# An attention decode kernel on one core: the output projection's weight in 1 MB blocks, two of them ahead of the last V piece

## The chip, the cores and the metric

The kernel runs on one core of a Trainium2 chip. The metric is device time in microseconds (us), lower is better. One execution of each kernel was also recorded by the hardware profiler; its span is about 1.7 us shorter than the time that is scored (the kernel before: span 1354.6 us, scored 1356.3 us in that run). All times inside a trace count from the start of the span. The engines are named as the profile names them: PE multiplies matrices (PEld is its loading of weights), DVE, ACT and POOL do the rest of the arithmetic, SP issues the transfers; DMA are the 16 engines that move the data. A block of "1 MB" is 2^20 bytes; the profile's own MB are decimal.

## The reference

Cut to what matters: a gated mix of a cached attention step and a small feed-forward block, for 4 tokens (D = 1024, 32 heads of 128, 8192 cached keys).

```python
g = sigmoid((x * gate_w).sum(-1, keepdims=True))
q = (x @ wq).reshape(B, 1, 32, 128).transpose(0, 2, 1, 3)
p = softmax(einsum("bhqd,bhkd->bhqk", q, k_cache) * 128 ** -0.5)   # k_cache: 4 x 32 x 8192 x 128 bf16
o = einsum("bhqk,bhkd->bhqd", p, v_cache)
a = o.reshape(B, 1, 4096) @ wo                                     # wo: 4096 x 1024 bf16, 8 MB
out = g * a + (1 - g) * b                                          # b: the feed-forward block
```

K and V are 256 MB each. Everything is read once, 575.7 MB in all, and little is computed on it.

## The kernel before

All large loads go through one ring of five SBUF slots of 4 MB. A load may start when the slot's earlier user is done. SP issues all of them, in program order.

```python
ring = ctx.enter_context(tc.tile_pool(name="ring", bufs=5))

def slot():
    return ring.tile([P, RING], BF, name="piece", tag="piece")

def wo_piece(g0, g1, r0=0, r1=FR):            # blocks g0..g1 of wo; one block is 1 MB, 8 matmuls of 512 columns
    ng, nr = g1 - g0, r1 - r0
    w = slot()[:, :ng * nr * D].rearrange("p (g r n) -> p g r n", g=ng, r=nr)
    nc.sync.dma_start(out=w.rearrange("p g r n -> p g (r n)"),
                      in_=wov[:, g0:g1, r0:r1].rearrange("p g r n -> p g (r n)"))
    def use():
        for g in range(ng):
            for r in range(nr):
                for n in range(NH):
                    mm_acc(acc[:, n * NB:(n + 1) * NB], LT[:, r0 + r, g0 + g, :], w[:, g, r, n * NB:(n + 1) * NB])
    return use
...
for u in range(NT + LAG):                      # NT = 64 pairs of heads, LAG = 4
    if u < NT:
        k_piece(u)
    if u >= LAG:
        v_piece(u - LAG)                       # the last V piece is fetched in four quarters
    ...
    if u == NT:
        o_rows(0, GE)                          # GE = 6: LT for wo blocks 0 to 5 is ready early
        add_x()
GS = NWB // 2                                  # NWB = 8 blocks
last = [wo_piece(0, GS), wo_piece(GS, GE), wo_piece(GE, NWB - 1),
        wo_piece(NWB - 1, NWB, 0, FR - 1), wo_piece(NWB - 1, NWB, FR - 1, FR)]
flush()                                        # the last heads: oT, OT
o_rows(GE, NWB)                                # LT for blocks 6 and 7 needs the last V piece
for use in last:
    use()
# then acc goes to SBUF in two halves (DVE, ACT) and out in two small DMAs
```

`acc` is the PSUM tile in which the output is summed, and `LT` holds the attention's result, transposed to be the weights of the wo matmuls. So wo comes as pieces of 4, 2, 1, 0.75 and 0.25 MB, all behind the last V piece, and PE's first wo matmul waits for all of the 4 MB.

## Time and profile before

| | before |
|---|---|
| time, median of 4 runs | 1355.85 us (1355.29 to 1356.14) |
| span of the profiled run | 1354.6 us |
| last landing of the last V piece | 1325.4 us |
| landing of the 4 MB wo piece | 1335.4 us |
| last wo landing | 1345.3 us |
| last matmul ends | 1351.7 us |

First from the page of the kernel before, the slices of DMA (the mean busy share of the 16 DMA engines in tenths, 40 equal slices), and its DMA queues (packets, MB, share of the 16 engines' span):

```profile
DMA  9999999999999999999999999999999999999996
...
q1 hardware_dynamic: 21904, 575.69, 99.0%
q8 instruction: 40, 0.66, 0.2%
```

The DMA engines are busy from end to end (99.0% of the span on q1). What can be won without moving fewer bytes lies where PE still works after the data has come. The timeline of PE in the kernel before shows that end (start us, us, engine, line, operation, out<-in, partitions x elements, count, and the idle time before it with what ended it). L342 are the last V matmuls, L355 and L232 the softmax tail, L150 the wo matmuls:

```profile
1325.63 3.19 PE L342 MATMUL o_ps<-piece,PB_143 128*8 128x512 bf16 x14
1329.54 1.06 PE L355 MATMUL oT<-selg,OS_139 128*128 128x8 f32 x8 [0.72 <-ACT OS_139 L348]
1330.93 0.33 PE L232 MATMUL o_ps<-OT,identb 128*32 128x8 bf16 x16 [0.33 <-DVE OT L358]
1335.42 16.26 PE L150 MATMUL acc<-piece,LT 128*4 128x512 bf16 x64 [4.16 <-DMA piece<-in_A_wo_dram]
```

PE waits 4.16 us for the 4 MB piece and then runs 64 matmuls in one go for 16.26 us. Windows of 2 us of the same stretch (busy time and instruction count of PE, PEld, DVE, ACT, POOL, then the granted PE clock, the DMA share and GB/s):

```profile
1332.00:1334.00 2.00, 0.00 (x0) 0.00 (x0) 0.00 (x0) 0.00 (x0) 0.00 (x0) 0.81 1.02 426
1334.00:1336.00 2.00, 0.58 (x2) 0.21 (x2) 0.00 (x0) 0.00 (x0) 0.00 (x0) 0.50 1.00 416
1336.00:1338.00 2.00, 2.00 (x7) 0.57 (x5) 0.00 (x0) 0.00 (x0) 0.00 (x0) 0.50 0.90 373
1338.00:1340.00 2.00, 2.00 (x6) 0.57 (x5) 0.00 (x0) 0.00 (x0) 0.00 (x0) 0.50 0.69 285
1340.00:1342.00 2.00, 2.00 (x10) 0.77 (x9) 0.00 (x0) 0.00 (x0) 0.00 (x0) 0.98 0.56 227
...
1346.00:1348.00 2.00, 2.00 (x11) 0.77 (x9) 0.00 (x0) 0.00 (x0) 0.00 (x0) 1.00 0.00 0
```

Two things are to be seen. The clock is at 0.50 from 1334 to 1340 us, so only 9 matmuls start from 1336 to 1340 us, one every 427 ns, where 18 start from 1344 to 1348, one every 216 ns (the counts in the windows are higher, because they include matmuls that reach in from the window before). And from 1346 us on nothing is fetched any more (DMA share 0.00) while PE works on until 1351.7.

The DMA share falls by steps from 1336 us on (0.90, 0.69, 0.56), long before the last byte. The reason shows in the records of completion. In this trace every large transfer has 16 such records, and they are spread out. I read them as one from each of the 16 DMA engines; a record does not name its engine, but the share of 0.56 from 1340 to 1342 us is that of nine busy engines of 16. Read so, these are the times at which engines were done with the last V quarter and the 4 MB piece, in us:

```
last V quarter   first 1317.3   seventh 1320.4   eighth 1323.8   last 1325.4
4 MB of wo       first 1327.3   seventh 1330.3   eighth 1333.8   last 1335.4
```

Seven engines are done 5 to 8 us before the slowest. The transfer has landed for PE when the slowest engine is done with it: the last record of the 4 MB is at 1335.4 us, and the first matmul on them starts at 1335.42.

### The profile page before, as it was taken

How to read it: one execution, taken by the hardware profiler on the slowest of the kernel's cores; microseconds unless marked ns; L12 is line 12 of the kernel's file. 1: busy time of each engine (PE TensorE's matmuls, PEld its weight loads, DVE VectorE, ACT ScalarE, POOL GpSimd, SP SyncE). 2: the span in 40 equal slices, each digit the busy share in tenths (PEclk: the TensorE clock that was granted, in tenths of full speed). 3: DMA queues.
4: the chain of work that ended last, by engine and by line, in shares of the span. 5: the costliest groups of instructions: out<-in, count | busy, mean ns of one | idle time of the engine just before them, and what ended most of it. 6: DMA issues, size and time to landing. Idle time of an engine off the chain costs nothing.

```text
span 1354.6 us, 11809 instructions
## 1 busy us (share of the span) xinstructions
PE 1065.1 (79%) x5112; PEld 434.5 (32%) x5112; DVE 622.3 (46%) x403; ACT 71.0 (5%) x118; POOL 86.8 (6%) x326
## 2 busy tenths in 40 slices
PE   2775888888687878879787777868877787888797
PEld 2432333333233323333233333323333332333333
DVE  1553345544543554455355534545454445445500
ACT  0000000000000000000000000000000000000010
POOL 2000000000000000000000000000000000000000
PEclk9877998889899988989999898989989888998898
DMA  9999999999999999999999999999999999999996
GB/s 403 429 431 430 425 430 432 432 432 431 429 432 430 433 430 431 427 431 432 431 433 432 433 428 432 430 428 433 431 433 430 432 428 430 432 431 433 432 419 258
DMA packets 21976, 576.46 MB, mean 426 GB/s; under 512 B 2322, under 2 KB 2330, under 8 KB 2596
## 3 DMA queue, kind: packets, MB, share of 16 engines
q1 hardware_dynamic: 21904, 575.69, 99.0%
q8 instruction: 40, 0.66, 0.2%
q14 instruction: 12, 0.10, 0.0%
q10 hardware_dynamic: 20, 0.02, 0.0%
HBM read 575.69 MB, written 0.01 MB: 425 GB/s over the span
## 4 chain that ended last, share of the span: by engine, by line
DMA 47%; PE 31%; DVE 12%; issue 7%; POOL 2%; ACT 1%; DVEq 0%; SPq 0%; ACTq 0%
DMA piece<-in_A_k_cache_dram 45%; PE o_ps L342 16%; PE S_ps L286 12%; DVE T L279 10%; DMA piece<-in_A_wo_dram 3%; PE acc L150 2%; PE oT L355 1%; DVE PT L311 1%; PE shr L150 1%; POOL PB_142 L316 1%; POOL PB_143 L316 1%; POOL tot L320 0%; ACT OS_138 L348 0%; ACT OS_139 L348 0%; DVE OT L358 0%
## 5 line engine op out<-in xcount | busy, mean ns | idle before, releaser
L279 DVE STREAM_TRANSPOSE T<-piece 128x2048 uint32<-128x2048 uint32 x256 | 576.1, 2288 | 474.7 <-DMA piece<-in_A_k_cache_dram 370.0
L286 PE MATMUL S_ps<-T,Z_140 128*128 128x512 bf16 x1024 | 287.9, 436 | 164.9 <-DVE T L279 164.6
L286 PE MATMUL S_ps<-T,Z_141 128*128 128x512 bf16 x1024 | 259.1, 401 | 84.1 <-DVE T L279 83.8
L342 PE MATMUL o_ps<-piece,PB_143 128*8 128x512 bf16 x1024 | 226.5, 381 | 2.1 <-POOL PB_143 L316 2.1
L342 PE MATMUL o_ps<-piece,PB_142 128*8 128x512 bf16 x1024 | 226.2, 379 | 0.0
L286 PEld LDWEIGHTS <-Z_140 128*128 128x128 bf16 x1024 | 111.3, 109 | 337.2 <-issue 256.4
L286 PEld LDWEIGHTS <-Z_141 128*128 128x128 bf16 x1024 | 102.1, 101 | 239.8 <-issue 143.6
L342 PEld LDWEIGHTS <-PB_143 128*8 128x8 bf16 x1024 | 86.5, 87 | 139.9 <-issue 15.3
L342 PEld LDWEIGHTS <-PB_142 128*8 128x8 bf16 x1024 | 86.4, 87 | 137.3 <-issue 13.6
L358 DVE SCALAR_TENSOR_TENSOR OT<-oT,sgb,rinv 128x8 bf16<-128x8 f32 x16 | 3.8, 236 | 126.0 <-PE oT L355 126.0
L270 POOL COPY Z_141<-qa 32x4 bf16<-32x4 bf16 x128 | 25.1, 196 | 525.1 <-PE S_ps L286 519.5
L270 POOL COPY Z_140<-qa 32x4 bf16<-32x4 bf16 x128 | 25.1, 196 | 496.4 <-PE S_ps L286 482.5
L348 ACT COPY OS_138<-o_ps 8x512 f32<-8x512 f32 x32 | 18.5, 577 | 594.2 <-PE o_ps L342 594.2
L348 ACT COPY OS_139<-o_ps 8x512 f32<-8x512 f32 x32 | 18.5, 577 | 536.8 <-PE o_ps L342 536.8
L150 PE MATMUL shr<-xw,piece 128*128 128x4 bf16 x704 | 22.6, 170 | 2.8 <-DMA piece<-in_A_wq_dram 2.6
L150 PEld LDWEIGHTS <-piece 128*128 128x128 bf16 x704 | 22.6, 113 | 3.9 <-DMA piece<-in_A_wq_dram 2.7
L150 PE MATMUL acc<-piece,LT 128*4 128x512 bf16 x64 | 16.3, 421 | 4.2 <-DMA piece<-in_A_wo_dram 4.2
L322 DVE RECIPROCAL rinv<-tot 128x8 f32<-128x8 f32 x16 | 3.2, 203 | 25.6 <-POOL tot L320 25.6
L355 PE MATMUL oT<-selg,OS_139 128*128 128x8 f32 x64 | 8.5, 259 | 5.7 <-ACT OS_139 L348 5.7
L355 PE MATMUL oT<-selg,OS_138 128*128 128x8 f32 x64 | 8.5, 259 | 5.7 <-ACT OS_138 L348 5.7
L316 POOL COPY PB_143<-PT 64x512 bf16<-64x512 bf16 x8 | 8.3, 1032 | 65.9 <-DVE rex L318 65.9
L150 PE MATMUL acc<-piece,hT 128*4 128x512 bf16 x56 | 12.4, 379 | 0.0
(99 smaller groups left out, 145.9 us busy)
## 6 DMA issues: line engine op xcount, KB each, us to landing
piece<-in_A_k_cache_dram SPq DMA_DIRECT2D x64, 4096.0 KB, 39.7
piece<-in_A_v_cache_dram SPq DMA_DIRECT2D x63, 4096.0 KB, 38.7
piece<-in_A_wq_dram SPq DMA_DIRECT2D x2, 4096.0 KB, 13.5
piece<-in_B_w_gate_dram SPq DMA_DIRECT2D x2, 3584.0 KB, 39.9
piece<-in_B_w_up_dram SPq DMA_DIRECT2D x2, 3584.0 KB
piece<-in_B_w_down_dram SPq DMA_DIRECT2D x1, 4096.0 KB, 39.9
piece<-in_A_v_cache_dram SPq DMA_DIRECT2D x4, 1024.0 KB, 38.4
piece<-in_A_wo_dram SPq DMA_DIRECT2D x1, 4096.0 KB, 39.4
```

The source lines that it names most:

```text
L150: nc.tensor.matmul(out_ap, lhsT=lhsT, rhs=rhs, start=start, stop=True, skip_group_check=True)
L270: nc.gpsimd.tensor_copy(out=Z[32 * a:32 * a + 32, :, 31 + 32 * a:32 + 32 * a], in_=qa[32 * a:32 * a + 32, :, h0 + a // QH, b:b + 1])
L279: nc.vector.transpose(out=T[:].rearrange("p j h i e -> p (j h i e)").bitcast(U32), in_=kn[:, c * CJ * Dh:(c + 1) * CJ * Dh].bitcast(U32))
L286: nc.tensor.matmul(sps[:, :], lhsT=Z[:, he, s:s + P], rhs=T[:, 16 * jl:16 * jl + 16, half, :, e], start=(t == 0 and jc == 0 and he == 0), ...
L311: nc.vector.transpose(out=PT[:].rearrange("p j i -> p (j i)"), in_=PTs[:])
L316: nc.gpsimd.tensor_copy(out=B_[W:P, :, :, 1, :], in_=Pv[W:P])
L322: nc.vector.reciprocal(out=rinv[:], in_=tot[:])
L342: nc.tensor.matmul(o_ps[32 * t:32 * t + NM, :], lhsT=B_[:, JC * t + jc, uq].rearrange("p s j -> p (s j)"), rhs=vn[:, j0 * Dh:(j0 + 4) * Dh ...
L348: nc.scalar.copy(out=o_sb[32 * t:32 * t + NM, :], in_=o_ps[32 * t:32 * t + NM, :])
L355: nc.tensor.matmul(oT[:, :], lhsT=o_sb[:, q * Dh:(q + 1) * Dh], rhs=selg[:, q].rearrange("p t s -> p (t s)"), start=(q == 0), stop=(q == 3))
L358: nc.vector.scalar_tensor_tensor(out=OT[:, hg:hg + GH, b], in0=oT[:, :], scalar=sgb[:, 1, b:b + 1], in1=rinv_t.pop(g)[:], op0=ALU.mult, op ...
```

## The change

The intent: wo comes in blocks of 1 MB, each waited for by its own 8 matmuls alone, so that matmuls start with the first block and run while later ones land; and two blocks go ahead of the last V piece, so that their 16 matmuls run before V's.

```diff
@@ -377,9 +377,11 @@
         if u == NT:
             o_rows(0, GE)
             add_x()
-    GS = NWB // 2
-    last = [wo_piece(0, GS), wo_piece(GS, GE), wo_piece(GE, NWB - 1),
-            wo_piece(NWB - 1, NWB, 0, FR - 1), wo_piece(NWB - 1, NWB, FR - 1, FR)]
+        if u == NT + LAG - 2:
+            for g in range(2):
+                wo_piece(g, g + 1)()
+    last = [wo_piece(g, g + 1) for g in range(2, NWB - 1)]
+    last += [wo_piece(NWB - 1, NWB, 0, FR - 1), wo_piece(NWB - 1, NWB, FR - 1, FR)]
     flush()
     o_rows(GE, NWB)
     for use in last:
```

The bytes, the 64 matmuls and the size of one contiguous run in DRAM (8 KB) stay. There are nine wo transfers in place of five.

## The prediction

> **What bounds the kernel.** The DMA queues. The slices show DMA at 0.9 or more in 39 of 40 slices; windows of the trace give 412 GB/s in 0–50 us and 430 GB/s from 100 to 1330 us, and 575.7 MB have to come. PE (79% busy) and DVE (46%) wait for data. The change moves the same bytes, so it can win only in the tail, where PE still works after the data has come.
>
> **The tail before, from timeline, waits and landings.** The last V piece's four quarters land at 1317.7, 1320.5, 1323.0 and 1325.4 us; the five wo pieces at 1335.4 (4 MB), 1340.3, 1342.8, 1344.6 and 1345.2 us. PE finishes V at 1328.8 and the last softmax rows at 1331.3, waits 4.2 us for the 4 MB piece (waits: "PE acc <- DMA wo", 4.2 us), then runs 64 matmuls from 1335.4 to 1351.7, 6.4 us past the last landing. About twelve of them start every 427 ns, the rest every 213 ns: the clock windows show 0.50 from 1334 to 1340 us. [...] counted on the trace, windows busy under about 0.4 fell and those above stayed fast, with few exceptions; the one before this drop was busy 0.32. The output then takes 2.9 us, to 1354.6.
>
> **What the change does.** 64 matmuls and 8 MB stay. Four more issues cost SP 0.33 us each, off the path. Two 1 MB blocks go ahead of the last V piece, so V's quarters land about 5 us later (1 MB takes 2.4–2.5 us here): estimated 1322.6 to 1330.4. Their 16 matmuls (3.4 us) fill PE after the piece before, which ends near 1322.7. V should end near 1332.7, the softmax tail near 1335.2, with no 4 us gap, so the clock should stay full. From there each block needs 8 × 0.213 = 1.7 us of PE against 2.45 us of DMA. The blocks land near 1332.9, 1335.4, 1337.9, 1340.3, 1342.8, the last two near 1344.6 and 1345.3; PE catches up with the fourth or fifth block and ends about 1.2 us after the last landing, 1346.5. Output: +2.9, span 1349.4. That is 5.2 us of 1354.6: half of it the clock (12 × 0.21 = 2.6 us), half the overlap of matmuls with landings.
>
> **Buffers.** Five slots. One-MB blocks use up slots with a quarter of the bytes. The last V piece now waits for the third piece before it (freed at 1307, still 13 us of data queued); blocks 4 and 5 of wo wait for blocks 0 and 1; block 6 waits for the V piece (1333), the last two for blocks 2 and 3 (1337, 1339). The slow DMA engines need them from 1340 on; the fast ones, about 8 us ahead, may idle, harmlessly. So I expect no bubble on the slow ones.
>
> **Predicted:** 1351 us, 8 in 10 between 1349.3 and 1354.5. Faster by over 2%: 0.01; within 2%: 0.97; slower by over 2%: 0.02.
>
> **What would show it.** Last landing still 1345–1346; first wo matmuls before V's; last matmul within 1.5 us of the last landing; clock windows 1.00 from 1320 to 1346; no DMA share under 0.9 before about 1335.
>
> **What would make it wrong.** A window that falls on the softmax tail drops the clock: half-speed blocks need 3.4 us each against 2.45, and most of the gain goes. Or slots come free late (release signals, landing of the previous use), the slow engines starve, and the last landing moves out by as much. Nothing before 1285 us should change.

The passage that is cut told a rule of the clock that did not come from the traces of this case. It carried no term of the sum, which stands as written: last matmul 1346.5, output 2.9, span 1349.4. A window is a stretch of 3.413 us: in the traces of the kernels before and after, each record of the granted clock (0.50 or 1.00) lasts a whole multiple of that, but for the one that the end of the trace cuts short. The count meant is this one, of the kernel before from 60 us on: 37 windows at full clock were followed by one at 0.50, and in 34 of them PE was busy for at most 0.42 of the window; 279 were not, and in all of them it was busy for 0.42 or more.

## The result, and the profile after

| | before | after |
|---|---|---|
| time, median of 4 runs | 1355.85 us (1355.29 to 1356.14) | 1351.32 us (1351.15 to 1351.37) |
| span of the profiled run | 1354.6 us | 1349.4 us |
| last V quarter landed | 1325.4 us | 1330.2 us |
| last wo landing | 1345.3 us | 1345.2 us |
| last matmul ends | 1351.7 us | 1346.5 us |

The ratio is 0.9967 with a 95% interval of 0.995 to 0.9984. Ratios here are the mean time of one kernel's fast runs over that of the other's fast runs of the same rounds, so not quite the ratio of the medians quoted. The gain, 4.5 us by the medians and 5.2 us of span in the profiled runs, is clear of the spread of either kernel but far under 2%.

From the page of the changed kernel, the same two lines as before:

```profile
DMA  9999999999999999999999999999999999999997
...
q1 hardware_dynamic: 21968, 575.69, 99.4%
```

The timeline of PE in the changed kernel. The first two lines are wo matmuls of the blocks ahead of V, of which there are 16, started from 1322.12 to 1325.4 us; the rest is the same end as before:

```profile
1322.12 0.38 PE L150 MATMUL acc<-piece,LT 128*4 128x512 bf16 x1
1322.77 2.32 PE L150 MATMUL acc<-piece,LT 128*4 128x512 bf16 x10
...
1325.80 6.30 PE L342 MATMUL o_ps<-piece,PB_143 128*8 128x512 bf16 x27
1332.82 1.06 PE L355 MATMUL oT<-selg,OS_139 128*128 128x8 f32 x8 [0.72 <-ACT OS_139 L348]
...
1334.54 5.12 PE L150 MATMUL acc<-piece,LT 128*4 128x512 bf16 x23
1340.21 1.89 PE L150 MATMUL acc<-piece,LT 128*4 128x512 bf16 x8 [0.55 <-DMA piece<-in_A_wo_dram]
1342.69 3.78 PE L150 MATMUL acc<-piece,LT 128*4 128x512 bf16 x16 [0.59 <-DMA piece<-in_A_wo_dram]
```

V and the softmax tail come about 3.3 us later than before, but the 4.16 us wait is gone. PE has caught up with the transfers at 1340 us: from there it does 8 matmuls in 1.9 us and waits twice more, 0.55 and 0.59 us, for the blocks that follow. Windows of the changed kernel, same columns as before:

```profile
1332.00:1334.00 2.00, 1.16 (x9) 1.07 (x9) 0.09 (x1) 0.58 (x1) 0.00 (x0) 1.00 0.98 352
1334.00:1336.00 2.00, 1.80 (x24) 0.84 (x24) 0.34 (x2) 0.00 (x0) 0.00 (x0) 1.00 0.97 406
1336.00:1338.00 2.00, 2.00 (x11) 0.77 (x10) 0.00 (x0) 0.00 (x0) 0.00 (x0) 1.00 0.82 301
1338.00:1340.00 2.00, 1.67 (x8) 0.59 (x7) 0.00 (x0) 0.00 (x0) 0.00 (x0) 1.00 0.88 353
1340.00:1342.00 2.00, 1.79 (x8) 0.67 (x8) 0.00 (x0) 0.00 (x0) 0.00 (x0) 1.00 0.79 325
1342.00:1344.00 2.00, 1.41 (x8) 0.51 (x7) 0.00 (x0) 0.00 (x0) 0.00 (x0) 1.00 0.52 210
1344.00:1346.00 2.00, 1.99 (x10) 0.74 (x9) 0.00 (x0) 0.00 (x0) 0.00 (x0) 1.00 0.13 48
1346.00:1348.00 2.00, 0.48 (x3) 0.00 (x0) 0.68 (x1) 0.57 (x1) 0.00 (x0) 1.00 0.01 4
```

The clock stays at 1.00, and PE is done about 1.3 us after the last landing. The landings, that is the last of the sixteen completion records of each transfer, in us, beside what the prediction had estimated:

```
                      V quarters                        blocks 2 to 6                              block 7 (two parts)
predicted    1322.6           ...      1330.4    1332.9  1335.4  1337.9  1340.3  1342.8    1344.6  1345.3
measured     1322.7  1325.2  1327.7   1330.2    1332.7  1335.1  1337.6  1340.2  1342.7    1344.6  1345.2
```

Three landings of the kernel before stand a little early in the prediction: its 1317.7, 1344.6 and 1345.2 are 1318.0, 1344.7 and 1345.3 when all sixteen records are counted. Nothing in its sum hangs on that.

### The profile page after: what moved, and what is told of

Read it like the earlier page. It is cut to its first block, busy times and chain, and to the rows that moved or that the text cites. A ratio compares the mean times of both kernels' runs of the same rounds, so it can differ in the third digit from the quotient of the medians.

```text
span 1349.4 us, 11817 instructions
## 1 busy us (share of the span) xinstructions
PE 1065.0 (79%) x5112; PEld 434.1 (32%) x5112; DVE 622.4 (46%) x403; ACT 71.0 (5%) x118; POOL 86.2 (6%) x326
## 4 chain that ended last, share of the span: by engine, by line
DMA 47%; PE 31%; DVE 11%; issue 8%; POOL 2%; ACT 1%; SPq 0%; DVEq 0%; ACTq 0%
DMA piece<-in_A_k_cache_dram 45%; PE o_ps L342 16%; PE S_ps L286 12%; DVE T L279 10%; DMA piece<-in_A_v_cache_dram 2%; PE oT L355 1%; PE acc L150 1%; DMA piece<-in_A_wo_dram 1%; DVE PT L311 1%; POOL PB_143 L316 1%; POOL PB_142 L316 1%; PE shr L150 1%; POOL tot L320 0%; ACT OS_138 L348 0%; ACT OS_139 L348 0%
```

## The experiments

Twelve kernels were run, in three batches. Those of a batch ran on the same chip and share their runs of the kernel before (medians 1356.65, 1355.93 and 1355.89 us; the first chip's runs of it fell in two groups, 1355.5 to 1355.8 and 1356.6 to 1356.9).

The theory: the gain is that PE's matmuls run while later transfers land, and that without the 4 us wait PE's clock does not drop; the last landing, set by the DMA engines, does not move. Rivals: the gain comes from the two blocks ahead of V; it is all clock, or no clock; it takes blocks as small as 1 MB.

### e1_split_only: all blocks behind V

Against the changed kernel:

```diff
-        if u == NT + LAG - 2:
-            for g in range(2):
-                wo_piece(g, g + 1)()
-    last = [wo_piece(g, g + 1) for g in range(2, NWB - 1)]
+    last = [wo_piece(g, g + 1) for g in range(0, NWB - 1)]
```

> All wo in 1 MB blocks, none ahead of the last V piece. My theory (the gain is that matmuls run while later blocks land, and that no 4 us gap drops the clock; the place of the two blocks does not matter): after the softmax tail at 1331.3 us two or three blocks have already landed, PE starts them at once at full clock, needs 64 x 0.213 = 13.6 us, i.e. could end at 1345, so it ends behind the last landing (1345.2) just as the changed kernel does: last matmul 1346.5, about 1351.3 us. Rival (the gain needs the two blocks ahead of V, which fill PE while it waits for V): 16 matmuls come back behind V, 3.4 us, about 1354.7 us.

Measured: 1351.16 us (1351.11 to 1351.27), span 1349.4. The theory holds, the rival falls: the place of the two blocks is worth nothing that shows. The PE timeline of e1_split_only has 47 wo matmuls in one run from 1331.74 us and then waits for blocks:

```profile
1331.74 10.30 PE L150 MATMUL acc<-piece,LT 128*4 128x512 bf16 x47
1342.64 3.77 PE L150 MATMUL acc<-piece,LT 128*4 128x512 bf16 x16 [0.59 <-DMA piece<-in_A_wo_dram]
```

By 1331.7 us two blocks lie there already, PE needs 1.7 us a block against 2.45 us between landings, and it has caught up before the last blocks. Here blocks 5 to 7 are issued as late as 1333.4 to 1338.6 us, because they wait for the slots of blocks 0 to 3. The fast DMA engines stood idle for that, as I read the records: the 16 of block 5 lie within 1.3 us (1338.8 to 1340.1) in place of 8. The last landing is at 1345.1 all the same. That was the prediction's "may idle, harmlessly".

### e2_ahead_only: two blocks ahead, a 4 MB piece behind

Against the changed kernel:

```diff
-    last = [wo_piece(g, g + 1) for g in range(2, NWB - 1)]
+    last = [wo_piece(2, GE), wo_piece(GE, NWB - 1)]
```

> The changed kernel with the two 1 MB blocks still ahead of V, but blocks 2 to 5 again as one 4 MB piece. My theory (waiting for a large piece is what costs): the 4 MB land at 1340.3, PE has waited 5 us and is at half clock again, 48 matmuls take about 12.8 us from there: last matmul near 1353, span 1356, about 1357.5 us, i.e. worse than the kernel before. Rival (what counts is having 16 matmuls fewer behind V): 1352.4 us.

Measured: 1357.47 us (1357.03 to 1357.93), ratio 1.0011. As expected, and by the medians slower than the kernel before, though the interval (0.9997 to 1.0025) still holds 1. From the PE waits of e2_ahead_only (engine, what it waited for, us in total, times, longest), and its timeline:

```profile
PE acc L150 <- DMA piece<-in_A_wo_dram: 5.6, 1, 5.6
```

```profile
1340.15 12.34 PE L150 MATMUL acc<-piece,LT 128*4 128x512 bf16 x48 [5.58 <-DMA piece<-in_A_wo_dram]
```

Sixteen matmuls fewer behind V do not help while the next matmul waits for four blocks at once: the 4 MB are complete only at 1340.1 us, 4.7 us later than in the kernel before, since the two blocks went first as well.

### e4_one_cut: the kernel before with one cut

Against the kernel before:

```diff
-    last = [wo_piece(0, GS), wo_piece(GS, GE), ...
+    last = [wo_piece(0, 2), wo_piece(2, GS), wo_piece(GS, GE), ...
```

> The kernel before with its 4 MB wo piece cut in two pieces of 2 MB, nothing else. My theory: the first 2 MB land near 1330.4, so PE has work at 1331.3 and stays at full clock; pieces land at 1330.4, 1335.4, 1340.3, 1342.8, 1344.6, 1345.2; 16 matmuls of 3.4 us after the third end at 1343.7, then 8, 6 and 2 more: last matmul near 1347.1, span 1350.0, about 1351.9 us, i.e. nearly all of the gain. Rival (it takes 1 MB blocks, each waited for alone): a good part of the gain is missing, 1353.5 us or more.

Measured: 1351.88 us (1351.76 to 1352.92). The time is the expected one to a tenth of a microsecond: this one cut of the 4 MB piece gives nearly all of the gain, 0.7 us less than e1_split_only on the same chip. Not everything went as in the sum, though. The profiled run was the slowest one (1352.92), and in it V ended 1.7 us later than expected and the clock did drop for one window, as its windows show (columns as before):

```profile
1328.00:1332.00 4.00, 3.28 (x19) 1.61 (x18) 0.00 (x0) 0.58 (x1) 0.00 (x0) 1.00 1.02 426
1332.00:1336.00 4.00, 3.67 (x27) 1.43 (x27) 0.43 (x2) 0.00 (x0) 0.00 (x0) 0.58 1.00 416
```

The other three runs, 1351.76 to 1351.97, have only a mean clock for the whole run, which can't show one window. They fit the sum without a drop; whether they had none is not shown.

### e5_ahead4 and e6_ahead6: more blocks ahead

Against the changed kernel, with 6 for 4 in e6_ahead6:

```diff
-            for g in range(2):
+            for g in range(4):
-    last = [wo_piece(g, g + 1) for g in range(2, NWB - 1)]
+    last = [wo_piece(g, g + 1) for g in range(4, NWB - 1)]
```

> Four 1 MB blocks ahead of the last V piece instead of two. My theory: V's quarters land 5 us later still (last near 1335.2), V's softmax tail ends near 1339.8, four blocks are left (32 matmuls, 6.8 us), PE ends near 1346.5 again: 1351.3 us, no change against two blocks. The last V piece then waits for the slot of the V piece before it (free at 1322.7) with the slow DMA engines having data until about 1325: if the issue comes too late for them, the last landing moves out from 1345.2 by the difference. Rival (more blocks ahead is better): under 1350.5 us.

Measured: 1352.98 us (1352.78 to 1353.81). Neither the theory's 1351.3 nor the rival's gain. Two things in the trace were not in the sum. The clock was at 0.50 for one window behind the softmax tail (1340.0 to 1343.4 us), and block 7 landed late: fifteen engines were done with its first part by 1344.6 us, one at 1345.5.

> Six blocks ahead of the last V piece, so only blocks 6 and 7 behind it. My theory: V lands last near 1340.2, its softmax tail ends near 1344.9, 16 matmuls (3.4 us) are then left: last matmul 1348.3, span 1351.2, about 1353.1 us, 1.8 us worse than two blocks ahead, with the last landing still at 1345-1346. Rival (more blocks ahead is better): under 1351 us.

Measured: 1353.54 us (1353.08 to 1354.56). As the theory has it: the softmax tail is done at 1345.1 and 16 matmuls follow, with the last one done at 1348.8. Block 7 landed late here too (1346.4 and 1346.9), but the matmuls of block 6 covered that: the 16 run without a gap.

So two blocks ahead of V do no harm that shows, and more of them do. With six, V's softmax tail has moved to the end; the loss with four has other causes, taken up under e10_ahead4_warm.

### e0_after_again and e7_small_tail: the last transfers smaller

e0_after_again is the changed kernel again, the yardstick of this batch.

> The changed kernel again, on the chip of the other three: 1351.3 us, last wo landing at 1345.2, last matmul end at 1346.5. It is the yardstick for the others of this call.

Measured: 1351.30 us (1351.14 to 1351.43), ratio 0.9965. Its profiled run (1351.39 us) happened to catch the risk that the prediction had named, a clock drop behind the softmax tail. Timeline and windows of e0_after_again:

```profile
1334.72 11.99 PE L150 MATMUL acc<-piece,LT 128*4 128x512 bf16 x47
```

```profile
1332.00:1336.00 4.00, 2.95 (x33) 1.87 (x32) 0.42 (x2) 0.58 (x1) 0.00 (x0) 0.97 0.94 371
1336.00:1340.00 4.00, 4.00 (x13) 1.24 (x11) 0.00 (x0) 0.00 (x0) 0.00 (x0) 0.60 0.82 297
1340.00:1344.00 4.00, 4.00 (x21) 1.57 (x19) 0.00 (x0) 0.00 (x0) 0.00 (x0) 1.00 0.73 295
```

The clock was 0.60 on average from 1336 to 1340 us. PE then worked without a wait and was done at 1346.7, 0.2 us later than in the profile with the full clock. The drop takes one window of 3.4 us, about half of which, 1.7 us, is lost (an estimate: in the kernel before, wo matmuls start every 427 ns at a clock of 0.50 and every 216 ns at 1.00); but without the drop PE stands waiting for blocks anyway (0.55 and 0.59 us in the timeline of the changed kernel), and the drop mostly eats those waits. Which of the two happens was luck: the activity of PE (the share of a window in which matmul columns stream, defined in the last section) was 0.41 in the window over the softmax tail here (1332.3 to 1335.8 us) and 0.43 in the changed kernel's first profile (1330.6 to 1334.0 us), where the clock stayed. By this count it hangs on where the windows of 3.4 us happen to fall.

e7_small_tail fetches blocks 6 and 7 into one slot, in smaller parts. Against the changed kernel, cut:

```diff
-    last = [wo_piece(g, g + 1) for g in range(2, NWB - 1)]
-    last += [wo_piece(NWB - 1, NWB, 0, FR - 1), wo_piece(NWB - 1, NWB, FR - 1, FR)]
+    last = [wo_piece(g, g + 1) for g in range(2, NWB - 2)]
+    tail = slot()[:, :2 * FR * D].rearrange("p (g r n) -> p g r n", g=2, r=FR)
+    def tail_piece(i, r0, r1):
+        nc.sync.dma_start(out=tail[:, i, r0:r1], in_=wov[:, NWB - 2 + i, r0:r1])
+        ...                                   # use(): the matmuls of rows r0 to r1 of block 6 + i
+    last += [tail_piece(0, 0, 2), tail_piece(0, 2, 4)] + [tail_piece(1, r, r + 1) for r in range(FR)]
```

> The changed kernel with wo blocks 6 and 7 in one slot, fetched as two transfers of 512 KB and four of 256 KB. My theory (PE has a backlog of 0.7 us at the last landing because block 7 comes as 6 + 2 matmuls): PE now ends with the last two matmuls 0.6 to 0.7 us after the last landing in place of 1.3, so 0.6 us less, about 1350.7 us. Rival (small transfers cost more than they save, the last landing moves out): 1351.3 us or more.

Measured: 1350.79 us (1350.64 to 1351.36), ratio 0.9963. The last landing was at 1345.4, and the last matmul ended at 1346.0, 0.6 us later. The theory holds; it is 0.5 us better than the changed kernel on the same chip, so this version beats both kernels, by little. One of its five runs lies inside the changed kernel's range.

### e3_before_warm and e9_before_warm2: the clock alone

Both put 18 matmuls with a dead result into the kernel before, to keep PE busy in its 4.1 us wait. The first:

```diff
     o_rows(GE, NWB)
+    for _ in range(18):
+        nc.tensor.matmul(shr[0:Bn, :], lhsT=identb[:, 0:Bn], rhs=qa[:].rearrange("p e h b -> p (e h b)"),
+                         start=True, stop=True, skip_group_check=True)
     for use in last:
```

> The kernel before, with 18 matmuls to a dead PSUM tile (their result is not used) in PE's 4.1 us wait for the 4 MB piece; same transfers. My theory of two halves: the clock stays at 1.00, the 64 matmuls take 13.8 us in place of 16.3, span 1352.1, about 1353.3 us; the other 2 us of the gain (overlap with the landings) stay missing. Rival 1 (it is all clock): 1351.3 us. Rival 2 (the clock plays no part, only the overlap): 1355.8 us.

Measured: 1356.03 us (1355.69 to 1356.66), as before, but it tells nothing: the order of the instructions shows that the framework's scheduler moved the 18 matmuls to an early place in the program, where their inputs were ready: they ran from 105.2 to 111.9 us. The second try takes `lhsT=LT[:, 0, GE, :]`, which is written only by the softmax tail.

> The kernel before, with 18 matmuls into a dead PSUM tile in PE's 4.1 us wait for the 4 MB piece (in the first try the scheduler had moved them to the start of the program; now their weights are the last rows' LT tile, so they can't start earlier). Transfers unchanged. Theory of two halves: the clock stays at 1.00 from 1331 to 1350 us, 64 matmuls take 13.8 us, last matmul near 1349.1, about 1353.3 us, 2.5 us better than before; the other 2 us of the change's gain stay missing. Rival 1 (it is all clock): 1351.3 us. Rival 2 (only overlap counts): 1355.9 us.

Measured: 1355.59 us (1354.46 to 1357.27). The runs spread over 2.8 us, so no verdict can rest on the time, and the theory's 1353.3 was not reached. The profiled run was the slowest. Its timeline shows why:

```profile
1333.37 5.43 PE L386 MATMUL shr<-qa,LT 128*4 128x512 bf16 x18 [0.32 <-DVE LT L234]
1338.63 13.98 PE L150 MATMUL acc<-piece,LT 128*4 128x512 bf16 x64
```

In this run the filler took 5.43 us, where 18 matmuls of 216 ns take 3.9: as I read it, the clock had dropped before the filler, and part of it ran at half speed. It held back the wo matmuls, which could have started at 1335.3. What the run does show is the cost of 64 wo matmuls at full clock: 13.98 us, 218 ns each, where the kernel before took 16.26. The clock's part is thus 2.3 us, measured as a duration. A run in which it alone is taken away did not succeed.

### e10_ahead4_warm and e11_small_tail_warm: filler behind V

e10_ahead4_warm is e5_ahead4 with five dead matmuls behind the last V matmul (`v_tiles[-1]` is the last V piece):

```diff
+    for _ in range(5):
+        nc.tensor.matmul(shr[0:Bn, :], lhsT=identb[:, 0:Bn], rhs=v_tiles[-1][:, RING - 4 * Dh:],
+                         start=True, stop=True, skip_group_check=True)
     flush()
     o_rows(GE, NWB)
```

> Four blocks ahead of V again, plus five matmuls into a dead PSUM tile between the last V matmul and the softmax tail, reading the last V quarter, in time where PE was idle. Theory (the 1.7 us that four blocks ahead lost came from one clock window at 0.50 behind the softmax tail, whose matmul activity was 0.34): activity of that window goes over 0.45, the clock stays at 1.00, last matmul near 1346.5, 1351.3 us. Rival (V's later end itself costs it, by PE having too little time left): 1353.0 us, as without them.

Measured: 1352.74 us (1351.84 to 1353.95). The clock did stay at 1.00, and yet the time came out near the rival's. The timeline of e10_ahead4_warm shows what took its place:

```profile
1339.94 5.13 PE L150 MATMUL acc<-piece,LT 128*4 128x512 bf16 x23
1346.11 1.89 PE L150 MATMUL acc<-piece,LT 128*4 128x512 bf16 x8 [1.04 <-DMA piece<-in_A_wo_dram]
```

PE now waits 1.04 us for block 7, which lands at 1346.1: fifteen engines were done by 1344.9, one 1.2 us later. In e5, e6 and e10 the last V piece is issued late, at 1322.5, 1325.8 and 1323.2 us, the DMA share falls meanwhile (0.50 from 1322 to 1324 us in e10), and the engines run level afterwards (DMA share 1.01 from 1342 to 1344 us in e10, where the changed kernel has 0.52). The last packet on the instruction queue comes at 1343.0, 1344.3 and 1343.6 us in these three, 1.1 us long, in the middle of the last transfers; in the changed kernel it came at 1337.9. That this packet is what held back the one engine is my reading. The records do not name the engine. So the loss of four blocks ahead has two causes, either of which is enough for most of it: with the clock's drop removed, the late landing remained.

e11_small_tail_warm is e7_small_tail with the same five matmuls.

> The version with the small last transfers (1350.8 us) plus the same five matmuls. Theory: that version is at full clock in most runs already; a cold window costs it little, as it cost the changed kernel 0.3 us in one profiled run. So the median stays at 1350.7 to 1350.8 us, and the spread (0.7 us) shrinks to about 0.4. Rival (the clock still costs something in most runs): 1350.4 us or less.

Measured: 1350.79 us (1350.74 to 1351.08). As expected: same median as e7_small_tail, with a spread of 0.34 us.

### e8_fewer_pe_instr: what sets the last landing

In every version with all its instructions but e5, e6 and e10, the last wo landing is between 1345.1 and 1345.4 us, and at the last V quarter the slowest engine is 8 us behind the fastest. What makes the slow engines lag? The queue list shows 40 packets, 0.66 MB, 16 KB each, on a queue called instruction, and PE has 10,224 (5112 weight loads and 5112 matmuls) of the trace's 11,809 instructions. The guess is that these packets bring PE's instructions. To test it, this kernel computes a wrong result, with half of PE's instructions and all transfers unchanged. Against the changed kernel:

```diff
-                for he in range(4):
+                for he in range(1):            # K: one matmul of four
-            for uq in range(4):
+            for uq in range(0, 4, 2):          # V: one of two
```

> Wrong result on purpose: of the K matmuls only one in four, of the V matmuls one in two, all transfers unchanged; 5120 of PE's 10224 instructions are gone. Theory (the 40 packets of 16 KB on the instruction queue, about 1.06 us each, are PE's instructions being fetched; they sit on some of the DMA engines, which therefore lag the others by 8 us at the end and set the last landing): 20 packets are left, the lag of the slowest engine behind the fastest at the last V quarter falls from 8.0 us to about 5.4, the last wo landing moves from 1345.2 to about 1342.6, about 1348.7 us. Rival (the lag is a property of the engines, the instruction fetch plays no part): last landing still at 1345.2, 1351 us.

Measured: 1349.61 us (1348.96 to 1350.38). From the page of e8_fewer_pe_instr, the DMA queues:

```profile
q1 hardware_dynamic: 21968, 575.69, 99.5%
q8 instruction: 20, 0.33, 0.1%
```

Half the packets are gone, the last wo landing moved to 1342.9 us, and from 97 us on the lag of the slowest engine grew about half as fast. The lag of the slowest behind the fastest engine at a 4 MB transfer or the last V quarter, in us:

```
landing near          97     456     828    1208    last V quarter
before               1.9     3.6     6.2     8.0     8.1
e8_fewer_pe_instr    2.1     3.0     3.5     5.4     5.5
```

The data packets themselves did not get faster: the median of a 32 KB packet is 1.215 us in both. From 97 to 1285 us, 42 of them took over 1.5 us in the kernel before, with e8 23. And these long ones are found where instructions are fetched: from 50 us on, 34 of the 37 instruction packets of the kernel before overlap in time with one, and 16 of the 17 of e8. So the growth of the lag is mostly PE's own instruction fetch, 40 packets of about 1.06 us; on which engines they ran the records do not say. The first 2 us of lag, at 97 us, are the same in both kernels and stay unexplained. The time fell by less than the landing, 1.7 against 2.3 us, because PE with half its work was at half clock much of the time (mean granted clock 0.70) and ended 1.8 us after the last landing.

### All runs

| kernel | wo transfers | median us | range us |
|---|---|---|---|
| before | 4, 2, 1, 0.75, 0.25 MB behind V | 1355.85 | 1355.29 to 1356.14 |
| changed | two 1 MB ahead, 1 MB blocks behind | 1351.32 | 1351.15 to 1351.37 |
| e1_split_only | none ahead, 1 MB blocks | 1351.16 | 1351.11 to 1351.27 |
| e4_one_cut | none ahead, 2, 2, 2, 1 ... MB | 1351.88 | 1351.76 to 1352.92 |
| e5_ahead4 | four ahead | 1352.98 | 1352.78 to 1353.81 |
| e10_ahead4_warm | four ahead, filler | 1352.74 | 1351.84 to 1353.95 |
| e6_ahead6 | six ahead | 1353.54 | 1353.08 to 1354.56 |
| e2_ahead_only | two ahead, 4 MB behind | 1357.47 | 1357.03 to 1357.93 |
| e3_before_warm | as before, filler misplaced | 1356.03 | 1355.69 to 1356.66 |
| e9_before_warm2 | as before, filler | 1355.59 | 1354.46 to 1357.27 |
| e0_after_again | as changed | 1351.30 | 1351.14 to 1351.43 |
| e7_small_tail | as changed, last 2 MB in six parts | 1350.79 | 1350.64 to 1351.36 |
| e11_small_tail_warm | the same, filler | 1350.79 | 1350.74 to 1351.08 |
| e8_fewer_pe_instr | as changed, half of PE's instructions | 1349.61 | 1348.96 to 1350.38 |

## Why the prediction was right

- **What bounds the kernel.** Said: the DMA queues; the change can win only behind the last landing. Shown: the last landing is at 1345.3 us before and 1345.2 after, and the matmuls behind it shrank from 6.3 to 1.3 us.
- **V's delay.** Said: quarters at 1322.6 to 1330.4, V ends near 1332.7, the softmax tail near 1335.2. Measured: 1322.7 to 1330.2, 1332.1 and 1334.5. The 4.16 us wait is gone, as said.
- **The end.** Said: last matmul 1346.5, span 1349.4, time 1351. Measured: 1346.5, 1349.4, 1351.32. Three things carried that: landing times per transfer were read from the trace and moved by whole blocks of 2.45 us; the matmuls were costed at 0.213 us each, where the traces show 0.216; and the slots were followed one by one, to see that no issue came too late.
- **Half clock, half overlap.** Said: 2.6 us each. The clock's part measured 2.3 us, as the difference of 16.26 and 13.98 us for the same 64 matmuls; the remaining 2.9 us of span are overlap by subtraction. But the two parts don't simply add, which the prediction didn't see: in e0_after_again's profile the clock did drop, and PE was done only 0.2 us later, so nearly all of the gain was there with the drop. The clock costs 2.3 us where all 64 matmuls run behind the data. No run showed the clock's part alone: two tries failed.
- **The clock.** Said: with no 4 us gap it should stay full. It did in the changed kernel's first profile, by luck: the window over the softmax tail had an activity of 0.43, and in e0_after_again, the same kernel, one of 0.41 was followed by a drop. The time came out right either way.
- **The two blocks ahead.** The prediction costed them as 16 matmuls that fill PE, and left open whether the gain needs them. It doesn't: without them 1351.16 us. The gain is from cutting what the first matmul waits for, and one cut of the 4 MB piece gives nearly all of it.
- **The step that was wrong: the size of the risk.** Said: if a clock window falls on the softmax tail, "half-speed blocks need 3.4 us each against 2.45, and most of the gain goes". It did fall there in one profiled run, and cost 0.2 us at the last matmul. The step took half speed to last; in fact it lasted one window, in which PE was busy without a gap (4.00 us of 4.00 from 1336 to 1340 us; see the last section), and most of the 1.7 us lost came out of waits that PE would have had. It may cost more where no such waits are left: e4_one_cut's run with a drop was 1 us above its others, but V ended 1.7 us late in it as well, and which of the two cost the 1 us is not shown.
- **Buffers.** Said: the fast engines may idle, harmlessly. Right up to two blocks ahead, shown by e1_split_only, where they idled most. With four and six ahead, V's issue comes so late that the engines run level, and one engine then finished late in the last landings; that a fetch of instructions held it up is my reading, not shown.

## What to carry to other kernels

At the end of a transfer-bound kernel, look at the first consumer's wait: cut what it waits for so that it starts as soon as anything has come (here a wait of 4.16 us went), and let the pieces shrink towards the end (e7_small_tail, 0.5 us); two pieces can be nearly as good as four (e4_one_cut 1351.88 us, e1_split_only 1351.16). Order between independent streams mattered less than this here, until the stream with the longest dependent tail came too late (e6_ahead6, 1353.54). To predict such a change, read each transfer's landing from the trace, move it by the bytes put before it, and follow each slot's release; in this kernel such sums met the measured time within 0.5 us in the change and in e1, e2, e4, e6, e7 and e11, and missed it by 0.9 to 2.3 us in e5, e8, e9 and e10, where the clock or one late engine was not in the sum or not where it put them.

## What the traces show beside it

- The clock. A window that is followed by a drop need not be idle in these traces. Take as activity the share of a full-clock window of 3.413 us in which matmul columns stream: 512 columns count 0.213 us, half of the 427 ns that lie between two starts at a clock of 0.50. Columns of fp32 operands are weighted by four, a choice of mine that no trace shows (the four fp32 matmuls of 512 columns from 1307.2 us on in the kernel before start 430 ns apart, twice the 215 of bf16). In the profiles of all kernels but e8, from 60 us on, 485 full-clock windows that were followed by a drop had at most 0.41, and 3601 that were not had at least 0.36; the kernels before and after have 73 of the one kind, at most 0.39, and 558 of the other, at least 0.37. Windows at 0.50 in these two: in 51 that were followed by another, columns streamed for at most 0.76 of the window, in 73 that were followed by the full clock for at least 0.83.
- The order of matmuls. In the changed kernel's trace the first three wo matmuls started at 1322.12, 1322.34 and 1322.55 us, each within 0.006 us of a V matmul, while three V matmuls that stand before them in the program started only at 1322.33, 1322.55 and 1322.77. The two groups write different PSUM partitions. In the kernel before, where wo had not come yet, all 16 matmuls of L232 start before the first wo matmul; in e4_one_cut, where it had, that one starts at 1332.73 and the last four of L232, which stand before it in the program, at 1332.74 and later.
- The fetch of instructions was not hidden here: 40 packets of 16 KB for 10,224 PE instructions, about 1.06 us each, and a lag of 8 us of the slowest engine behind the fastest at the end; 20 packets and 5.5 us with half the instructions. The packets that halve with PE's instructions are on queue 8; queue 14 has 12 instruction packets (0.10 MB) in the changed kernel and 13 in e8.
- The DMA engines were busy at 0.99 and more, and one split of a 4 MB transfer still gave 4 us (e4_one_cut), because it was the consumer that waited; the last landing stayed (1345.3 us before, 1345.2 with the split).
